# 64-row passes of three units in one group on a shared ring of six banks, with contiguous weight parts and an on-chip identity

## The chip, the cores and the metric

The kernel runs on one core of a Trainium2 chip. The core has four engines that compute: TensorE (PE in the profile; its weight loads have a row of their own, PEld), VectorE (DVE), ScalarE (ACT) and GpSimd (POOL). SyncE (SP) issues the transfers, which run on sixteen DMA engines. The metric is the device time of one execution in microseconds; lower is better.

## The reference

The input is x of 2048 tokens by 448 features. It is normalized per token, and the normalized xn feeds two branches whose results are added to x.

```
xn  = layernorm(x)                                   # no scale, no shift
A   = irfft2(rfft2(xn) * (w_r + 1j * w_i))           # 2048 x 448, filter 2048 x 225
g   = xn @ W_gate;  g = g * (g > 0)                  # W_gate, W_up: 448 x 1792
B   = (g * (xn @ W_up)) @ W_down                     # W_down: 1792 x 448
out = x + A + B
```

All inputs and the output are float32.

## The kernel before

**Precision.** Every matrix product is done in float16 on TensorE, with both operands split into a high and a low part. A product takes three kinds of pass: high by high, low by high and high by low. The weights are scaled by powers of two first, which come from their sums of squares (`w_sq`, then a reduction over the partitions on GpSimd in `w_sum`, then `w_scale`, then the split in `w_hi` and `w_lo`).

**Tokens.** Tokens are handled in four chunks q (order 0, 2, 1, 3) of 512. Each chunk's normalized rows lie transposed in a tile T of nine 128-row slices: three and a half slices of high part and as many of low part, since 448 is 3.5 times 128. The first chunk is transposed by TensorE against an identity (`ln_tp`, L338), the others by a transposing DMA (`ln_dma`, L332).

**The gated branch.** The 1792 hidden features are 14 slabs f of 128, in groups of 5, 5 and 4. A unit is one pair (f, q): gate and up for 128 features and 512 tokens, accumulated over the 3.5 slices. That is 20 passes over 128 rows (`gu_full`, L714) and, for the last half slice, two passes over 64 rows (`gu_half`, L721): the up one uses rows 64 to 127 of the array, the gate one rows 0 to 63. Passes of the two row halves can run side by side. Units are therefore taken in pairs: the first unit of a pair runs its 20 full passes, then four half passes follow, two that open its mate and two that finish itself (`gu_halves`), and then the mate runs its 20 full passes. After each unit `gu_post` empties the banks: ScalarE takes the rectified gate (`gu_relu`, L751), VectorE multiplies it by up (`gu_times`, L755), ScalarE and VectorE split the product into high and low (L759, L763). When all units of a group and a chunk are done, four down rounds follow (`dn_mm`, L782), each of 128 tokens and three passes per slab; VectorE adds each to the result (`dn_post`, L788).

**The banks.** The accumulators have eight banks: two tiles of two banks for gate and up (`gu`), two banks for down rounds (`dn`) and two for everything else (`fx`: transposes and Fourier passes).

**The spectral branch.** It is a list of background steps (`bg`): a Fourier transform over the features and one over part of the tokens as passes on TensorE (L360, L392), butterflies on VectorE, the filter, and all of it back (L611, L632). Between a spectrum's mirrored rows there are swaps through SBUF by DMA (L547, L548). Each step has a cost by a table in the kernel, and after each unit `run_bg` issues as many steps as a share of the unit's time allows. The share (`load`) is found by halving, such that all steps fit between the sixth unit and `last_gu`.

**What sets the order.** The opening, up to the first chunk's units, is a list of names written out by hand (`OPENING`), and each engine runs its part of it in that order. Names that matter here: `lx` loads a token tile in the normalization's layout, `lw` the next part of gate or up weights, `lid` the identity, `st` takes a tile's statistics (L256), `rs` computes the reciprocal deviation (L272 to L277), `wsc` the scale of a weight part, `hp` issues the half passes. After the opening a scheduler orders each engine's instructions ahead of the run by priority and by a modelled time; units are written in program order, posts with a raised priority. A tile of a ring takes a free bank, and an instruction that needs one waits until the bank's last reader is done.

Of the kernel before, what the change touches and what calls it, by code (L numbers as in the profile page):

```python
# [30 lines left out]
lx0 lx4 lw lid lw lx8 lx12 lw lw lw lw lx2 lx10 lx6 lx14 lwd0 lwd1 lwd2 lwd3 lwd4 warm st0 st4 sqA rsA hi4  # L31
xn4 xn0 wsqW0g0 cp4 st8 hi0 parW0g0 st12 wsqW0g1 cp0 tpA0 lo0 tpA4 kw1 wscW0g0 sqB tpB0 kw6 parW0g1 wsqW1g0
rsB whiW0g0 vevB0 lo4 wsqW1g1 xn12 tpB4 kw3 hi8 parW1 wscW0g1 xn8 whiW0g1 cp8 vevA0 vevA4 hi12 tpA8 vevB4
hh10 hh00 lo8 wsqW2g1 cp12 tpA12 hl00 lo12 aevA12 tpB8 aevA8 hl10 wloW0g0 lw aevB8 tpB12 wscW1 lh00 aevB12
wloW0g1 lw lfd hh01 hh11 whiW1g0 st2 lh01 lh10 whiW1g1 hl01 wloW1g0 lw hl11 wsqW2g0 cl0 cl4 wloW1g1 lw ly0 ly4 ly8
ly12 lh11 wsqW3g0 st10 parW2 hp0 st14 wsqW3g1 gu1g0 st6 wdq0 parW3 cl8 cl12 wscW2 sqC wscW3 whiW2g0 rsC gu1g1 re0
wloW2g0 whiW3g1 tm0 whiW2g1 xn6 wsqW4g0 xn2 gu2g0 dt0 dt4 wloW2g1 hi2 dt8 dt12 re1 xn10 gh0 wloW3g1 whiW3g0 tm1 gu2g1 wdq1
wloW3g0 hi10 xn14 lo2 hi14 hi6 cp14 hp2 wsqW4g1 cp2 lo6 gu3g0 cp10 cl2 dm2 lo14 re2 parW4 wdq2 cp6 wscW4 tm2
whiW4g0 cl14 dm14 lo10 wdq4 gu3g1 wloW4g0 gh1 cl10 dm10 gl0 whiW4g1 gl1 cl6 dm6 gu4g0 re3 wloW4g1 wdq3 tm3 wdp gh3
wdsc gh2 gu4g1 gl2 wdh1 wdh2 wdl1 wdh0 wdl2 hp4 gl3 re4 wdh3 tm4 wdl0 gh4 wdh4 gl4 wdl3 wdl4  # L40
# [37 lines left out]
def _constants():  # L78
# [57 lines left out]
    ident = np.eye(128, dtype=np.float16)  # L136
    return dict(ident=ident, c_fd=c_fd, c_fm=c_fm, c_im=c_im, c_row=np.ascontiguousarray(c_row),
# [4 lines left out]
def tile_gfnet_reglu(ctx: ExitStack, tc: tile.TileContext, x, xr, wgu, wd, wf, wrow, ident, c_fd, c_fm, c_im, c_row, c_id,  # L142
# [10 lines left out]
    def fx():  # L153
        return psum.tile([128, 512], F32, name="fx", bufs=2)
# [77 lines left out]
    def load_w(f, g, eng=nc.sync):  # L232
        wst[f, g] = mt([128, 4, 128], F32, "wst", 8)
        eng.dma_start(wst[f, g], wgu[f, :, g])
# [18 lines left out]
    def ln_stats(q, j):  # L253
        n2 = q + 4 * j
        st = ft([128, 6], F32, "bst", 2)
        V.bn_stats(st, xr_t[n2])  # L256
        if j == 0:
            mv[q] = ft([128, 4, 2], F32, "mv", 2)
        V.bn_aggr(mv[q][:, j, :], st)

    rst = {}
# [7 lines left out]
    def ln_rstd(q, js=(0, 1, 2, 3), bias=False):  # L269
        w, m = rst[q, js[0]]  # L270
        sd, r0, t, r, nm = (w[:, i] for i in range(5))
        V.reciprocal(r0, sd)  # L272
        V.scalar_tensor_tensor(t, m[:, :, 1], 1e-5, r0, op0=OP.add, op1=OP.mult)
        V.scalar_tensor_tensor(t, t, -0.5 * 2048, r0, op0=OP.mult, op1=OP.mult)
        V.scalar_tensor_tensor(r, t, 1.5 * 2048, r0, op0=OP.add, op1=OP.mult)
        if bias:
            V.scalar_tensor_tensor(nm, m[:, :, 0], -1.0, r, op0=OP.mult, op1=OP.mult)  # L277
        for i, j in enumerate(js):
            rst[q, j] = r[:, i:i + 1], nm[:, i:i + 1], m[:, i, 0:1]
# [10 lines left out]
    def ln_xn(n2):  # L290
        xn_b[n2] = free.pop(0)
        xn[n2] = xn_b[n2].rearrange("p g c k -> p (g c k)")[:, 0:D]
        r, _, mean = rst[n2 % 4, n2 // 4]
        V.tensor_scalar(xn[n2], xr_t[n2], mean, r, op0=OP.subtract, op1=OP.mult)

    def ln_hi(n2, fused=False):
        new_tt(n2)
        o = tt[n2].rearrange("p a b -> p (a b)")[:, 0:D]
        r, nm, _ = rst[n2 % 4, n2 // 4]
# [34 lines left out]
    def ln_tp(n2, tiles):  # L334
        if n2 not in tp:
            tp[n2] = fx().bitcast(F16).rearrange("p (a b) -> p a b", b=128)
# [11 lines left out]

    zps, eo, X, Xh, yps, cur = {}, {}, {}, {}, {}, {}

    def f_dft(n2):
        q, j = n2 % 4, n2 // 4
        js = slice(128 * j, 128 * (j + 1))
        ps = fx()
# [33 lines left out]
    def f_sdft(n2):  # L388
        y = yps[n2] = fx()[:, 0:XW].rearrange("p (g c k) -> p g c k", g=4, c=2)
# [177 lines left out]
    def row_dft(d):  # L567
        y = state["rowps"] = fx()
# [35 lines left out]
    def i_sdft(n2):  # L604
        ps = fx()
# [20 lines left out]
    def i_ddft(n2):  # L626
        ps = fx()
# [25 lines left out]

    def w_scale(f, gs=(0, 1)):
        sc = mt([128, 2], F32, "wsc", 6)
        e = eg[:, f, gs[0]:gs[-1] + 1]
        half_exponent(e, state["wm", f][:, 1, gs[0]:gs[-1] + 1])
        shift_exponent(sc[:, 0:len(gs)], e, -1, 188)
# [49 lines left out]
    def gu_open(f, q):  # L708
        hps[f, q] = psum.tile([128, 2, 512], F32, name="gu", bufs=2)

    def gu_full(f, q, gs, cs, start, stop, seq=SEQ):
        for g in gs:
            for i, (a, b) in enumerate(seq):
                last["P"] = P.matmul(hps[f, q][:, g, cs], wt[f, g][:, a, :], Tq[q][:, b, cs],  # L714
                                     start=(start and i == 0), stop=(stop and i == len(seq) - 1)).ins

    def gu_half(f, q, g, start, prev):
# [3 lines left out]
        m = P.matmul(hps[f, q][:, g, 0:512], wt[f, g][rows, 7, :], Tq[q][rows, b, :], start=start, stop=not start).ins  # L721
# [7 lines left out]
    def gu_unit(f, q, mate):  # L729
# [7 lines left out]
        gu_halves(f, q, mate)  # L737
# [11 lines left out]
    def gu_relu(f, q):  # L749
        g1s[f, q] = mt([128, 512], F32, "g1", 3)  # L750
        last["A"] = A.activation(g1s[f, q], hps[f, q][:, 0, :], AF.Relu, scale=2.0 ** -22).ins  # L751

    def gu_times(f, q):
        g1 = g1s[f, q]
        last["V"] = V.scalar_tensor_tensor(g1, hps[f, q][:, 1, :], 2.0 ** -22, g1, op0=OP.mult, op1=OP.mult).ins  # L755
# [201 lines left out]
    gseq = [("gu", g, f, q) for g, fs in enumerate(groups) for q in CHUNKS for f in fs]  # L957
    units, pend = [], []
    for k, u in enumerate(gseq):
        units.append(u)  # L960
        if k % 2 and pend:
# [5 lines left out]
    mates = {u: v for u, v in zip(gseq[::2], gseq[1::2])}  # L967
# [222 lines left out]
```

## Time and profile before

| what | value |
|---|---|
| median of 3 runs | 448.41 us (447.95 to 448.84) |
| span of the profiled execution | 446.9 us |
| granted TensorE clock | 1.000 |
| moved by DMA | 39.66 MB, mean 89 GB/s |
| full gate and up passes, L714 | 1140 |
| half passes, L721 | 112 |
| down passes, L782 | 672 |

The profile is of one execution by the hardware profiler. Its page gives busy times of the engines, the span in 40 slices, the chain of work that ended last, followed back from the last instruction, and the costliest groups of instructions. In a group's line stands the source line, the engine, the operation, what it writes and reads, the count, then busy time, the mean length of one in ns, and the idle time of the engine just before. Further views are the chain in order of time, the waits (who waited for whom: total, times, longest), the timeline, and busy times by window. A TensorE pass's recorded length is longer than its distance to the next, as passes are pipelined; costs of passes are therefore read as distances or from the chain.

### The profile page before, as it was taken

Reading aid. Unit: us, or ns where it says so; the run is one execution under the profiler, and the core shown is the slowest. Engines: PE = TensorE matmul, PEld = TensorE weight load, DVE = VectorE, ACT = ScalarE, POOL = GpSimd, SP = SyncE. Lnnn points to the kernel's source line nnn. Section 1 sums busy time; section 2 is a strip of 40 time slices with the busy share of each in tenths; the row PEclk is TensorE's granted clock in tenths of the full one; section 3 lists DMA queues with packets and bytes.
Section 4 is the critical chain, followed back from the end, with each engine's and each line's share of the span. In section 5 each row is a group of like instructions: output and inputs, shape, how many; then the busy total and the mean of one; then the engine's idle time right before and its main releaser. Section 6 shows DMA issues by size and latency. Waiting matters only on the chain.

```text
span 446.9 us, 7057 instructions
## 1 busy us (share of the span) xinstructions
PE 437.4 (98%) x2618; PEld 217.6 (49%) x2618; DVE 373.0 (83%) x801; ACT 178.7 (40%) x365; POOL 35.5 (8%) x100
## 2 busy tenths in 40 slices
PE   7999999999999999999999999999999999999996
PEld 2543545444545444444444444444444456546564
DVE  5988696998859989899999999896997998656474
ACT  5886242451543666043224145434142242233230
POOL 2431031040000150000000010000000000000000
PEclk9999999999999999999999999999999999999999
DMA  7919976041001261431220021000001332121113
GB/s 243 362 38 266 359 243 118 1 94 38 0 14 61 96 219 37 129 103 64 82 77 11 1 83 54 0 13 0 14 0 42 106 96 74 54 76 53 64 43 123
DMA packets 36827, 39.66 MB, mean 89 GB/s; under 512 B 17799, under 2 KB 32185, under 8 KB 36793
## 3 DMA queue, kind: packets, MB, share of 16 engines
q1 hardware_dynamic: 36792, 39.21, 28.1%
q8 instruction: 20, 0.33, 0.3%
q14 instruction: 15, 0.11, 0.1%
HBM read 24.45 MB, written 3.67 MB: 63 GB/s over the span
## 4 chain that ended last, share of the span: by engine, by line
PE 84%; DVE 7%; DMA 4%; ACT 1%; issue 1%; POOL 1%; SPq 1%; DVEq 0%; ACTq 0%
PE gu L714 47%; PE dn L782 27%; PE gu L721 3%; PE fx L360 2%; PE fx L392 2%; DMA sw<-y 2%; PE fx L611 2%; PE fx L632 1%; DMA y<-in_xr 1%; DVE g L755 1%; DMA T<-tt 1%; DVE bst L256 1%; DVE wt L668 1%; DVE xy L788 1%; DVE y L553 1%
## 5 line engine op out<-in xcount | busy, mean ns | idle before, releaser
L714 PE MATMUL gu<-T,wt 128*128 128x512 f16 (+1 forms) x1140 | 256.1, 376 | 0.0
L714 PEld LDWEIGHTS <-wt 128*128 128x128 f16 x1140 | 108.6, 98 | 129.9 <-issue 9.3
L782 PE MATMUL dn<-wdt,h 128*128 128x448 f16 x672 | 136.4, 352 | 0.0
L782 PEld LDWEIGHTS <-h 128*128 128x128 f16 x672 | 64.8, 98 | 60.5
L751 ACT ACTIVATE g<-gu 128x512 f32<-128x512 f32 x56 | 33.2, 594 | 111.0 <-PE gu L721 75.3
L759 ACT ACTIVATE h<-g 128x512 f16<-128x512 f32 x56 | 35.0, 626 | 52.8 <-DVE g L755 52.7
L755 DVE SCALAR_TENSOR_TENSOR g<-gu,g 128x512 f32<-128x512 f32 x56 | 38.3, 684 | 10.3 <-ACT g L751 10.2
L788 DVE SCALAR_TENSOR_TENSOR xy<-dn,dsc,xy 128x448 f32<-128x448 f32 x48 | 32.5, 678 | 15.5 <-PE dn L782 15.3
L763 DVE TENSOR_TENSOR h<-g,h 128x512 f16<-128x512 f32 x56 | 38.2, 684 | 4.9 <-ACT h L759 4.8
L664 ACT ACTIVATE wt<-wst,wsc 128x512 f16<-128x512 f32 x28 | 19.1, 716 | 15.7 <-DVE wsc L204 15.7
L197 POOL PARTITION_ALL_REDUCE wm<-wm x15 | 7.9, 523 | 159.2 <-ACT junk L194 159.2
L668 DVE SCALAR_TENSOR_TENSOR wt<-wst,wsc,wt 128x512 f16<-128x512 f32 x28 | 20.4, 744 | 0.0
L637 DVE SCALAR_TENSOR_TENSOR xy<-fx,fsc,xy 128x448 f32<-128x448 f32 x16 | 10.8, 679 | 10.1 <-PE fx L632 10.1
L721 PE MATMUL gu<-T,wt 64*128 64x512 f16 x112 | 17.0, 381 | 1.7 <-DVE g L755 0.8
L399 DVE TENSOR_TENSOR y<-y 128x456 f32<-128x456 f32 x22 | 13.9, 630 | 4.7 <-DMA row<-y 4.5
L194 ACT ACTIVATE junk<-wst 128x512 bf16<-128x512 f32 x28 | 17.4, 622 | 0.3
L553 DVE TENSOR_TENSOR y<-y,sw 128x456 f32<-128x456 f32 x16 | 10.0, 626 | 8.5 <-DMA sw<-y 8.5
L595 ACT ACTIVATE vt<-y,fsc 128x912 f16<-128x912 f32 x8 | 8.4, 1052 | 20.7 <-PE fx L611 12.3
L618 ACT ACTIVATE wf<-fx 114x512 f16<-114x512 f32 x16 | 9.4, 587 | 17.2 <-PE fx L611 17.0
L398 DVE TENSOR_TENSOR y<-y 128x456 f32<-128x456 f32 x22 | 13.8, 626 | 0.2
L611 PEld LDWEIGHTS <-vt 128*128 128x128 f16 x192 | 12.0, 98 | 3.3
L611 PE MATMUL fx<-wf,vt 128*128 128x128 f16 x192 | 13.2, 219 | 0.0
(115 smaller groups left out, 430.6 us busy)
## 6 DMA issues: line engine op xcount, KB each, us to landing
sw<-y SPq DMA_DIRECT2D x32, 224.4 KB
wst<-in_wgu SPq DMA_DIRECT2D x28, 256.0 KB
wf<-in_wf SPq DMA_DIRECT2D x8, 456.0 KB
y<-in_xr SPq DMA_DIRECT2D x16, 224.0 KB
xy<-in_x SPq DMA_DIRECT2D x16, 224.0 KB
out<-xy SPq DMA_DIRECT2D x16, 224.0 KB
wdst<-in_wd SPq DMA_DIRECT2D x14, 224.0 KB
fm<-in_c_fm SPq DMA_DIRECT2D x8, 128.0 KB
```

The costliest lines, as they stand in the source:

```text
L194: A.activation(o, src, AF.Square, scale=SQ, accum_out=acc)
L611: P.matmul(o, v[:, h, w], m[:, c, :], start=(i == 0), stop=(i == 2), skip_group_check=True)
L664: A.activation(w[:, 0:4, :], wst[f, g], AF.Copy, scale=wsc[f, g])
L668: V.scalar_tensor_tensor(w[:, 4:8, :], st, sc, w[:, 0:4, :], op0=OP.mult, op1=OP.subtract)
L714: last["P"] = P.matmul(hps[f, q][:, g, cs], wt[f, g][:, a, :], Tq[q][:, b, cs], start=(start and i == 0), stop=(stop and i == len(seq) - 1 ...
L721: m = P.matmul(hps[f, q][:, g, 0:512], wt[f, g][rows, 7, :], Tq[q][rows, b, :], start=start, stop=not start).ins
L751: last["A"] = A.activation(g1s[f, q], hps[f, q][:, 0, :], AF.Relu, scale=2.0 ** -22).ins
L755: last["V"] = V.scalar_tensor_tensor(g1, hps[f, q][:, 1, :], 2.0 ** -22, g1, op0=OP.mult, op1=OP.mult).ins
L759: A.activation(ht[f, q][:, 0, :], g1s[f, q], AF.Copy)
L763: V.tensor_tensor(h[:, 1, :], g1s.pop((f, q)), h[:, 0, :], op=OP.subtract)
L782: last["P"] = P.matmul(ps[:, 0:D], ht[f, q][:, a, js], wdt[f][:, b, :], start=(i == 0), stop=(i == n - 1)).ins
L788: last["V"] = V.scalar_tensor_tensor(xy[:, n2, :], dps[n2][:, 0:D], dsc[:, g:g + 1], xy[:, n2, :], op0=OP.mult, op1=OP.add).ins
```

## The change

It has four parts.

**Groups of six half passes.** The 56 units are cut into runs of two or three: two, two, sixteen times three, two, two. The first unit of a run opens all its mates: after its full passes come two half passes for each mate and two of its own. The down rounds of a group and a chunk are placed behind the first mate that follows. In the order of instructions, full passes that are issued after a group of half passes are kept behind it.

```diff
-    mates = {u: v for u, v in zip(gseq[::2], gseq[1::2])}
+    mates, inner, k = {}, set(), 0
+    for n in [2, 2] + [3] * 16 + [2, 2]:
+        mates[gseq[k]] = gseq[k + 1:k + n]
+        inner.update(gseq[k + 1:k + n])
+        k += n
...
-        if k % 2 and pend:
+        if u in inner and pend:
             units += pend
...
-    def gu_halves(f, q, mate):
-        gu_open(*mate)
+    def gu_halves(f, q, mates):
         m = last["P"]
-        for i in range(4):
+        vs = [v[2:] for v in mates] + [(f, q)]
+        for i in range(2 * len(vs)):
+            v = vs[i // 2]
+            if i % 2 == 0 and v != (f, q):
+                gu_open(*v)
+                opened.add(v)
             with tc.high_priority(offset=2000 if i else 0):
-                m = gu_half(*((f, q) if i > 1 else mate), 1 - i % 2, i < 2, m)
-        opened.add(mate)
+                m = gu_half(*v, 1 - i % 2, v != (f, q), m)
+        last["half"] = m
```

**A ring of six banks.** Gate and up take one bank each, and down rounds draw from the same six.

```diff
-    def fx():
-        return psum.tile([128, 512], F32, name="fx", bufs=2)
+    RINGS = {'gu': ('gu', 6), 'dn': ('gu', 6), 'fx': ('fx', 2)}
+
+    def bank(name="fx"):
+        tag, n = RINGS[name]
+        return psum.tile([128, 512], F32, name=name, tag=tag, bufs=n)
...
-        hps[f, q] = psum.tile([128, 2, 512], F32, name="gu", bufs=2)
+        hps[f, q] = [bank("gu") for g in range(2)]
...
-        ps = psum.tile([128, 512], F32, name="dn", bufs=2)
+        ps = bank("dn")
```

**Weights and identity.** The host lays gate and up out by slab and kind, so that one part (128 rows of 2 KB) is contiguous in HBM; before, gate and up rows alternated. The identity is no longer an input: GpSimd makes it behind the fill of the warm-up tile, and `lid` leaves the opening's list.

```diff
-        eng.dma_start(wst[f, g], wgu[f, :, g])
+        eng.dma_start(wst[f, g], wgu[f, g])
...
-    wgu = np.ascontiguousarray(np.stack([wtiles(B_W_gate), wtiles(B_W_up)], axis=2))
+    wgu = np.ascontiguousarray(np.stack([wtiles(B_W_gate), wtiles(B_W_up)], axis=1))
...
         G.memset(warm, 0.0)
-        wps = psum.tile([128, 512], F32, name="dn", bufs=2)
+        G.memset(id_t, 0.0)
+        G.affine_select(id_t, id_t, pattern=[[-1, 128]], compare_op=OP.not_equal, fill=1.0, base=0, channel_multiplier=1)
+        wps = bank("dn")
```

The entries `rs` and `wsc` of the opening are cut into single steps (`rsA.0` to `rsA.4`, `wscW0g0.0` and `.1` and so on), each step standing where the whole entry stood; apart from `lid` the order of the opening is the same. In the main part `w_scale` is cut in two likewise (`w_exp` and `w_scale`), both issued at the same unit.

**Pace.** Background steps must fit into two gate/up units fewer.

```diff
-    last_gu = max(gus) - 6
+    last_gu = max(gus) - 8
```

More of the change, by code (lines that the diff above doesn't have):

```diff
@@ L335, in ln_tp @@
         if n2 not in tp:
-            tp[n2] = fx().bitcast(F16).rearrange("p (a b) -> p a b", b=128)
+            tp[n2] = bank().bitcast(F16).rearrange("p (a b) -> p a b", b=128)
         for a in tiles:
@@ L353, in f_dft @@
         js = slice(128 * j, 128 * (j + 1))
-        ps = fx()
+        ps = bank()
         T = Tq[q]
@@ L567, in row_dft @@
     def row_dft(d):
-        y = state["rowps"] = fx()
+        y = state["rowps"] = bank()
         for d in ((0, 1), (2,))[d]:
@@ L604, in i_sdft @@
     def i_sdft(n2):
-        ps = fx()
+        ps = bank()
         v, m = vt[n2 % 8][:, n2 // 8], im_t[n2 % 8][:, n2 // 8]
@@ L626, in i_ddft @@
     def i_ddft(n2):
-        ps = fx()
+        ps = bank()
         h = pgh[n2]
@@ L713, in gu_full @@
             for i, (a, b) in enumerate(seq):
-                last["P"] = P.matmul(hps[f, q][:, g, cs], wt[f, g][:, a, :], Tq[q][:, b, cs],
+                m = last["P"] = P.matmul(hps[f, q][g][:, cs], wt[f, g][:, a, :], Tq[q][:, b, cs],
                                      start=(start and i == 0), stop=(stop and i == len(seq) - 1)).ins
+                if "opened" in state and "half" in last:
+                    tc.add_manual_dep(m, last["half"].name, NOSYNC, reason="half passes stand together")
     def gu_half(f, q, g, start, prev):
         rows, b = TOP[g]
-        m = P.matmul(hps[f, q][:, g, 0:512], wt[f, g][rows, 7, :], Tq[q][rows, b, :], start=start, stop=not start).ins
+        m = P.matmul(hps[f, q][g], wt[f, g][rows, 7, :], Tq[q][rows, b, :], start=start, stop=not start).ins
         if "opened" in state:
@@ L727, in tile_gfnet_reglu, with gu_unit @@
     opened = set()
-    def gu_unit(f, q, mate):
+    def gu_unit(f, q, mates):
         gs, cs = (0, 1), slice(0, 512)
@@ L1033, in tile_gfnet_reglu @@
             piece("sq" + tag, ln_sd, q, js)
-            piece("rs" + tag, ln_rstd, q, js, c == 0)
+            for i in range(4 + (c == 0)):
+                piece(f"rs{tag}.{i}", ln_rstd, q, js, c == 0, range(i, i + 1))
         for j in range(4):
@@ L1046, in gu_slab @@
     def gu_slab(f, g):
-        if f % 2 == 0 and g == 0:
+        first = ("gu", 0, f, q) in mates
+        if first and g == 0:
             gu_open(f, q)
-        gu_full(f, q, (g,), slice(0, 512), f % 2 == 0, f % 2 == 1)
+        gu_full(f, q, (g,), slice(0, 512), first, not first)
     for f in groups[0]:
@@ L1117, in tile_gfnet_reglu @@
             run_bg(until=marks["T", q])
-            gu_unit(f, q, (mates.get(u) or (0, 0, None, None))[2:])
+            gu_unit(f, q, mates.get(u))
         else:
```

78 lines of the change are left out of this document (38 added, 40 removed).

## The prediction

> **What bounds the kernel now.** All durations come from one profiled execution with a span of 446.9 us; the median of the runs is 448.41 us, so 1.5 us lie outside the span, and I leave them as they are. I read the page's busy times first, then its chain of work, and then asked what TensorE waits for.
>
> ```profile
> PE 437.4 (98%) x2618; PEld 217.6 (49%) x2618; DVE 373.0 (83%) x801; ACT 178.7 (40%) x365; POOL 35.5 (8%) x100
> PE 84%; DVE 7%; DMA 4%; ACT 1%; issue 1%; POOL 1%; SPq 1%; DVEq 0%; ACTq 0%
> ```
>
> TensorE is busy nearly throughout and carries 84% of the chain that ended last. A busy TensorE isn't yet one that streams densely, so the view of its waits comes next; of its seven rows these two are the only ones on the gate and up passes over 0.2 us:
>
> ```profile
> PE gu L721 <- DVE g L755: 0.8, 1, 0.8
> PE gu L721 <- DMA T<-tt: 0.8, 1, 0.8
> ```
>
> Both fall on the 64-row passes (L721). Everything else that can be won in the middle must therefore come from the passes themselves. The chain in order of time (start, length, what) shows what a group of four of them costs:
>
> ```profile
> 108.23 0.54 PE gu L721 x4
> 108.77 4.42 PE gu L714 x20
> 113.19 1.21 PE fx L360 x24
> 114.40 4.32 PE gu L714 x20
> 118.72 0.54 PE gu L721 x4
> 119.26 1.32 PE fx L360 x24
> ```
>
> Twenty full passes take 4.32 us, 0.216 us each. The same twenty take 4.42 us right behind a group, and the 24 Fourier passes 1.32 instead of 1.21 us: a change of row mode costs about 0.10 us more than the group's own 0.54 us. So a group costs 0.64 us, where its two pairs, each pair running side by side in the two halves of the array, need 2 x 0.216 = 0.43 us. The overhead is **0.21 us per group**. The timeline shows why:
>
> ```profile
> 118.65 0.11 PEld L721 LDWEIGHTS <-wt 64*128 64x128 f16 x4 [0.42 <-issue]
> 118.65 0.61 PE L721 MATMUL gu<-T,wt 64*128 64x512 f16 x4
> ...
> 119.18 0.47 PEld L360 LDWEIGHTS <-T 128*128 128x128 f16 x9 [0.42 <-issue]
> ```
>
> The weight load stands idle 0.42 us on entry and again on exit; elsewhere it runs ahead under the passes.
>
> **Part 1: three units in a group.**
>
> ```profile
> L721 PE MATMUL gu<-T,wt 64*128 64x512 f16 x112 | 17.0, 381 | 1.7 <-DVE g L755 0.8
> ```
>
> The 56 gate/up units make 112 such passes, 28 groups of four. By the list in the change (two twos, sixteen threes, two twos) they become 4 groups of four and 16 of six, again 112 passes. A group of six adds one pair: 0.64 + 0.22 = 0.86 us. Before: 28 x 0.64 = 17.9 us. After: 16 x 0.86 + 4 x 0.64 = 16.3 us. **Gain 1.6 us**, all of it on TensorE, which sets the end.
>
> The third pair's weights are the unknown. No row shows a third pair. One end: its loads hide, as do those of the second pair in the quoted timeline row (four loads in 0.11 us, all at the start) and those of the full passes. The other end: both loads stand bare, about the 0.11 us of that row, 16 x 0.11 = 1.8 us, which takes the gain away. I take nothing, because the second pair of the same mode is the nearest row.
>
> The Trainium skill, "TensorE: Matmul & The Clock Gate", section "Part 3: Packing small matmuls — row/col tiling", says that a weight load overlaps a running matmul only when it goes to another row group. By that rule the third pair could load nothing while the second pair fills both groups, and the sum would be that of rival A. The trace disagrees as far as it reaches: the second pair's loads are recorded beside the first pair's run.
>
> **Part 2: ring of six banks.** Before, gate and up shared a two-bank tile with two buffers, and the down passes had two banks of their own. Now both draw single banks from six. The gate bank comes free after L751 alone instead of after L755, and a down round may hold up to four banks. Against that, at each group of six all six banks belong to gate and up.
>
> ```profile
> L751 ACT ACTIVATE g<-gu 128x512 f32<-128x512 f32 x56 | 33.2, 594 | 111.0 <-PE gu L721 75.3
> ...
> L755 DVE SCALAR_TENSOR_TENSOR g<-gu,g 128x512 f32<-128x512 f32 x56 | 38.3, 684 | 10.3 <-ACT g L751 10.2
> L788 DVE SCALAR_TENSOR_TENSOR xy<-dn,dsc,xy 128x448 f32<-128x448 f32 x48 | 32.5, 678 | 15.5 <-PE dn L782 15.3
> ```
>
> The last unit of one group must be emptied (0.59 + 0.68 = 1.3 us) while the first unit of the next runs its 4.32 us, which leaves 3.0 us for queues. That is the same slack as now, and it failed once in 28 groups: VectorE stood behind a swap transfer, and the group waited 0.81 us.
>
> ```profile
> 397.66 0.63 DVE L553 TENSOR_TENSOR y<-y,sw 128x456 f32<-128x456 f32 x1 [4.27 <-DMA sw<-y]
> ...
> 398.75 0.69 DVE L755 SCALAR_TENSOR_TENSOR g<-gu,g 128x512 f32<-128x512 f32 x1
> ...
> 399.49 0.61 PE L721 MATMUL gu<-T,wt 64*128 64x512 f16 x4 [0.81 <-DVE g L755]
> ```
>
> What is queued behind such a wait is every later TensorE pass. I count no gain and no loss: the swap waits remain, there are fewer groups to hit, but each needs more banks. The bounds are -0.8 us (this wait goes) and the price of rival C.
>
> **Part 3: the opening.** The order written out by hand loses one entry, the load of the identity; splitting the rsqrt steps and the weight scale into several entries leaves their order as it was, so I cost that at nothing. The chain of the opening:
>
> ```profile
> 2.14 0.43 SPq L1022
> ...
> 2.62 0.43 SPq L234
> ...
> 3.09 4.74 DMA y<-in_xr
> ```
>
> The identity's issue (L1022) holds SyncE from 2.14 to 2.62 us. Without it the second weight part and the third and fourth token tiles are issued 0.48 us earlier. VectorE waits for that third tile:
>
> ```profile
> 7.85 0.63 DVE L256 BATCH_NORM_STATS2 bst<-y 128x6 f32<-128x448 f32 x1 [0.80 <-DMA y<-in_xr]
> ```
>
> ```profile
> 10.00:20.00 10.00, 9.00 (x80) 6.16 (x81) 9.66 (x32) 9.16 (x21) 3.51 (x10) 1.00 1.02 379
> ```
>
> It can win at most these 0.80 us, and at least nothing, if the transfers and not the issue set the landing. From there to 20 us VectorE is full (9.66 of 10 us in the second row), so a shift is handed on. Contiguous parts act on the same landing. In windows over the transfers (last two columns: DMA share, GB/s):
>
> ```profile
> 3.50:5.00 1.50, 1.50 (x5) 0.51 (x4) 1.32 (x4) 0.07 (x1) 0.00 (x0) 1.00 0.80 201
> ...
> 8.10:9.60 1.50, 0.72 (x7) 0.39 (x7) 1.43 (x5) 0.92 (x4) 0.78 (x3) 1.00 0.89 279
> 11.50:14.00 2.50, 1.65 (x14) 0.88 (x14) 2.47 (x10) 1.95 (x5) 0.99 (x3) 1.00 1.05 402
> 16.60:18.00 1.40, 1.40 (x15) 1.27 (x13) 1.33 (x4) 1.40 (x4) 0.00 (x0) 1.00 1.05 384
> ```
>
> Weight parts move at 201 and 279 GB/s in the first 10 us, at 384 at 16.6 us; the down weights and tokens at 402. Since strided parts reach 384 later, I put the early slowness down to starting up, not to the stride, and give contiguity nothing by itself. For the opening I take **0.4 us**, half of the bound and a little under the slot of 0.48.
>
> The identity now costs GpSimd two instructions behind the fill of the warm-up tile.
>
> ```profile
> 0.96 0.52 POOL L1077 MEMSET warm<- 128x512 f16 x1
> ...
> 7.06 0.22 POOL L307 COPY tt<-tt 128x48 f16<-128x48 f16 x1 [5.57 <-ACT tt L301]
> ...
> 8.32 0.51 PE L338 MATMUL fx<-id_t,tt 128*128 128x128 f16 x6 [0.85 <-ACT tt L301]
> ```
>
> A quarter of that fill is 0.13 us; the select has no row and lies between the copy's 0.22 and, for twice the fill, 1.0 us. GpSimd's idle 5.57 us hide both, and the first reader comes at 8.32. Without the cover TensorE's first transposes would wait by the excess.
>
> **Part 4: pace.** Background work is spread over two gate/up units fewer, by the kernel's own table about 2% more per unit. VectorE has no room for that in the middle:
>
> ```profile
> 190.00:200.00 10.00, 10.00 (x52) 4.48 (x50) 9.97 (x24) 4.65 (x8) 0.00 (x0) 1.00 0.30 96
> ...
> 420.00:430.00 10.00, 10.00 (x98) 6.16 (x97) 5.75 (x9) 4.00 (x7) 0.00 (x0) 1.00 0.07 24
> ```
>
> VectorE is busy 9.97 of 10 us there, 5.75 near the end, where TensorE is full anyway. So earlier background work shortens nothing by itself: what doesn't fit slides on, and gate/up evacuations have priority in the order. Nothing, with rival C as the bad end.
>
> **Sum:** 446.9 - 1.6 - 0.4 = 444.9 us of span, **446.4 us** as a time.
>
> **Rivals.**
>
> A, the third pair's weights aren't hidden: +1.8 us, so 448.2 us. For it: in these passes both row groups are occupied. Against it: the four loads in 0.11 us.
>
> B, the groups don't stay together, so the change doesn't do what it says. A group needs four banks for its two mates; if the second mate's aren't free when the first's are, the scheduler can set other passes between, and the row mode changes twice more, 0.21 us as worked out. Half of the sixteen broken costs 1.7 us: 448.1 us. All: 449.8. For it: only the first pass of a group has no raised priority, and the later ones need banks of their own now. Against it: the mates' banks are freed some 3 us before they are needed.
>
> C, slower: **down rounds in front of a group**. In the order of before, ten of the 28 groups stand right behind down passes; the first and the last of the ten in the timeline:
>
> ```profile
> 156.53 0.35 PE L782 MATMUL dn<-wdt,h 128*128 128x448 f16 x1
> 156.81 0.39 PE L721 MATMUL gu<-T,wt 64*128 64x512 f16 x2
> ...
> 363.30 0.54 PE L782 MATMUL dn<-wdt,h 128*128 128x448 f16 x2
> 363.77 0.39 PE L721 MATMUL gu<-T,wt 64*128 64x512 f16 x2
> ```
>
> On their own two banks that costs nothing; on the common ring the second mate waits until the last down bank is emptied, 0.68 us of L788 and what VectorE has in hand, some 1.0 us. TensorE stands, and all behind it. In proportion that would meet seven of 20 groups. Four of these waits give 446.4 + 4.0 = 450.4 us; from three on the kernel is slower. Against it: the new order is made for the new ring, and a down round now follows the second unit with a whole unit behind it.
>
> The Trainium skill, "TensorEngine Tiling (Array Packing)", section "Gotcha 1: PSUM Pressure", warns that row tiling raises the demand for PSUM banks. That speaks against six passes on six banks. The trace bears it out so far in one wait of 0.81 us in 28 groups.
>
> D, better: the wait at 399 us goes too and the opening gives its whole 0.80: 445.2 us.
>
> **Chances.** The forecast 0.53, D 0.10, A 0.07, B 0.13, C 0.17. A measurement of this kernel tells apart about 0.2%, 0.9 us: faster means below 447.5. The forecast and D lie there, B and A mostly within, C and a wholly broken B beyond. Faster 0.63, same 0.19, slower 0.18. The range runs from 444.6 (D, and the transposes' 0.8 us wait for T partly gone) to 449.8 (B whole, C with three waits), leaving out C's longer half and little below.
>
> **What would show it.** Right: 20 runs of L721 passes, sixteen of six in about 0.76 us each; 0.42 us idle of the weight load 40 times instead of 56; no wait at L721 on VectorE beyond one; the third token tile's statistics starting near 7.4 us; no load of the identity. Wrong: pairs of a six more than 0.23 us apart (A), L721 passes in more than 20 runs (B), L721 waiting on L788 (C), or statistics still at 7.85 us. If the opening moves but its gain is missing at 40 us, another wait took it: then the transposes' transfer into T is the first suspect.

## The result and the profile after

| what | before | after |
|---|---|---|
| median of the runs | 448.41 us (447.95 to 448.84) | 465.44 us (462.63 to 466.59) |
| ratio | | 1.037, interval 1.035 to 1.039 |
| span of the profiled execution | 446.9 us | 462.9 us |
| third group of half passes starts at | 38.87 us | 50.71 us |
| from there to the last TensorE pass | 404.04 us | 408.18 us |

The kernel became slower by 17 us, far outside the range. One execution in the whole study, the traced one of run f3 below, took 573.8 us at a granted clock of 0.754, and the ratios leave it out. The last two rows split the 16.0 us between the spans: 11.84 us are lost before the third group of half passes, 4.14 us after it. Lines have moved: half passes are L721 as before, but full passes are L712, down passes L786, gate times up L759, the transposes' copies on GpSimd L306.

The page of after, busy times and the chain by engine:

```profile
PE 439.7 (95%) x2618; PEld 220.3 (48%) x2618; DVE 375.6 (81%) x801; ACT 177.4 (38%) x365; POOL 40.1 (9%) x102
PE 63%; DVE 17%; DMA 8%; issue 6%; ACT 3%; SPq 2%; POOL 1%; DVEq 0%; ACTq 0%; POOLq 0%
```

TensorE falls from 98% to 95% of a longer span and from 84% to 63% of the chain. Its waits in after (who waits for whom: us in total, times, longest) say for whom:

```profile
PE fx L336 <- POOL tt L306: 8.6, 1, 8.6
PE fx L608 <- DVE wf L619: 3.1, 3, 1.9
PE fx L336 <- POOL id_t L1092: 2.6, 1, 2.6
PE gu L721 <- DVE g L759: 1.7, 1, 1.7
...
PE fx L357 <- DVE eo L369: 0.5, 1, 0.5
```

**The opening.** Two of these waits are on GpSimd, 8.6 and 2.6 us, together 11.2. GpSimd's timeline in after (start, length, instruction, idle time before it and what ended that):

```profile
1.42 0.20 POOL L1091 MEMSET id_t<- 128x128 f16 x1
9.96 0.28 POOL L1092 TENSOR_SCALAR_AFFINE_SELECT id_t<-id_t 128x128 f16<-128x128 f16 x1 [8.33 <-issue]
...
10.38 0.23 POOL L306 COPY tt<-tt 128x64 f16<-128x64 f16 x1
19.05 0.40 POOL L190 PARTITION_ALL_REDUCE wm<-wm  x1 [8.44 <-issue]
```

The select itself takes 0.28 us, but GpSimd stands still for 8.33 us in front of it and for 8.44 us in front of the first sum over partitions behind it. "issue" means that no semaphore ended the wait: GpSimd waited for nothing that the profile shows. Before, the same sum came after 0.25 us:

```profile
7.70 0.39 POOL L197 PARTITION_ALL_REDUCE wm<-wm  x1 [0.25 <-ACT junk L194]
```

Everything in the opening hangs on these two. VectorE needs the sum for the scale of the weights, TensorE the identity and GpSimd's copies for its transposes; after, VectorE and TensorE:

```profile
19.48 0.15 DVE L193 TENSOR_SCALAR eg<-wm 128x1 uint32<-128x1 uint32 x1 [9.91 <-POOL wm L190]
19.85 0.29 PE L336 MATMUL fx<-id_t,tt 128*128 128x128 f16 x1 [8.62 <-POOL tt L306]
```

The third group of half passes, in after:

```profile
50.71 0.82 PE L721 MATMUL gu<-T,wt 64*128 64x512 f16 x6 [1.16 <-DMA T<-tt]
```

It was at 38.87 us before. Windows of after (length; busy time and count for PE, PEld, DVE, ACT, POOL; granted clock; DMA share; GB/s) show the hole, and a clock that is lower through it and behind it:

```profile
10.00:20.00 10.00, 1.08 (x13) 0.79 (x13) 0.45 (x4) 0.15 (x1) 1.56 (x7) 0.61 0.74 274
20.00:30.00 10.00, 10.00 (x69) 6.76 (x68) 8.01 (x26) 7.35 (x15) 3.42 (x10) 0.71 0.27 77
```

**The groups of six.** They are what the prediction said. The chain of after in order of time:

```profile
260.85 4.32 PE gu L712 x20
265.17 0.75 PE gu L721 x6
265.92 13.06 PE gu L712 x60
```

Six half passes take 0.75 us; the sixty full passes behind them take 13.06 where 60 x 0.216 = 12.96, so 0.10 us of exit. With this exit a group of six costs 0.85 us, against 0.86 worked out. The trace has 20 groups, as planned.

**The middle.** The 4.14 us are these, by distances between starts of TensorE's passes:

| term | us |
|---|---|
| shorter groups (28 became 20), as predicted | -1.6 |
| the wait of before at 399 us is gone | -0.9 |
| one wait inside a group of six at 199 us | +2.0 |
| five stalls at Fourier passes (127, 368, 396, 406 and 407 us) | +4.5 |
| sum | +4.0 of 4.1 |

The longest of the five stalls, in after (VectorE's and TensorE's rows):

```profile
403.65 0.63 DVE L550 TENSOR_TENSOR y<-y,sw 128x456 f32<-128x456 f32 x1 [4.04 <-DMA sw<-y]
...
408.15 0.68 DVE L619 SCALAR_TENSOR_TENSOR wf<-fx,wf 114x512 f16<-114x512 f32 x1
...
408.89 0.84 PE L608 MATMUL fx<-wf,vt 128*128 128x128 f16 x12 [1.86 <-DVE wf L619]
```

VectorE takes its instructions in a fixed order. The butterfly at L550 waits 4.04 us for a swap transfer, and what follows stands almost without a gap until 408 us: the evacuations, the next inverse step and in the end L619, which empties a Fourier bank that TensorE needs. VectorE's waits on swaps, before and after:

```profile
DVE y L553 <- DMA sw<-y: 8.5, 3, 4.3
```

```profile
DVE y L550 <- DMA sw<-y: 14.6, 6, 4.0
```

### The profile page after: what moved, and what is told of

Read it like the earlier page. It is cut to its first block, busy times and chain, and to the rows that moved or that the text cites. A ratio compares the mean times of both kernels' runs of the same rounds, so it can differ in the third digit from the quotient of the medians.

```text
span 462.9 us, 7090 instructions
## 1 busy us (share of the span) xinstructions
PE 439.7 (95%) x2618; PEld 220.3 (48%) x2618; DVE 375.6 (81%) x801; ACT 177.4 (38%) x365; POOL 40.1 (9%) x102
## 4 chain that ended last, share of the span: by engine, by line
PE 63%; DVE 17%; DMA 8%; issue 6%; ACT 3%; SPq 2%; POOL 1%; DVEq 0%; ACTq 0%; POOLq 0%
PE gu L712 35%; PE dn L786 19%; DMA sw<-y 6%; PE gu L721 2%; DVE g L759 2%; PE fx L389 2%; PE fx L629 1%; DVE xy L792 1%; PE fx L357 1%; PE fx L608 1%; DVE y L551 1%; ACT junk L187 1%; DVE y L419 1%; SPq L330 1%; DMA row<-y 1%
## 5 line engine op out<-in xcount | busy, mean ns | idle before, releaser
L712 PE MATMUL gu<-T,wt 128*128 128x512 f16 (+1 forms) x1140 | 253.5, 376 | 0.0
L712 PEld LDWEIGHTS <-wt 128*128 128x128 f16 x1140 | 109.3, 98 | 128.8 <-issue 6.8
L786 PE MATMUL dn<-wdt,h 128*128 128x448 f16 x672 | 132.4, 353 | 0.0
L786 PEld LDWEIGHTS <-h 128*128 128x128 f16 x672 | 65.0, 98 | 59.4
L759 DVE SCALAR_TENSOR_TENSOR g<-gu,g 128x512 f32<-128x512 f32 x56 | 38.3, 684 | 10.9 <-ACT g L755 6.8
L550 DVE TENSOR_TENSOR y<-y,sw 128x456 f32<-128x456 f32 x16 | 10.0, 627 | 16.1 <-DMA sw<-y 14.6
L396 DVE TENSOR_TENSOR y<-y 128x456 f32<-128x456 f32 x22 | 13.8, 629 | 6.8 <-DMA row<-y 6.4
L721 PE MATMUL gu<-T,wt 64*128 64x512 f16 x112 | 16.1, 380 | 3.1 <-DVE g L759 1.7
L380 ACT ACTIVATE Xh<-X 128x912 f16<-128x912 f32 x8 | 7.7, 962 | 21.6 <-DVE X L378 21.6
L336 PE MATMUL fx<-id_t,tt 128*128 128x128 f16 x32 | 3.6, 244 | 11.2 <-POOL tt L306 8.6
## 6 DMA issues: line engine op xcount, KB each, us to landing
wf<-in_wf SPq DMA_DIRECT2D x8, 456.0 KB
```

Of the source, the lines that this page charges most:

```text
L712: m = last["P"] = P.matmul(hps[f, q][g][:, cs], wt[f, g][:, a, :], Tq[q][:, b, cs], start=(start and i == 0), stop=(stop and i == len(seq) ...
L721: m = P.matmul(hps[f, q][g], wt[f, g][rows, 7, :], Tq[q][rows, b, :], start=start, stop=not start).ins
L759: last["V"] = V.scalar_tensor_tensor(g1, hps[f, q][1], 2.0 ** -22, g1, op0=OP.mult, op1=OP.mult).ins
L786: last["P"] = P.matmul(ps[:, 0:D], ht[f, q][:, a, js], wdt[f][:, b, :], start=(i == 0), stop=(i == n - 1)).ins
```

## The experiments

Four questions: what the identity costs, whether the pace, the ring or the groups make the middle longer, whether it is instead any change of order at all, and whether the groups of six keep their gain. Beside the runs e, f, g and h, before was measured again on the same chip: 448.7, 448.6, 448.8 and 448.6 us. The ratio is taken over the executions, not from the two medians.

| label | kernel | median, us | ratio to before, interval |
|---|---|---|---|
| e1_after_loaded_identity | after, identity loaded | 453.76 | 1.0113 (1.0081 to 1.0145) |
| e2_before_made_identity | before, identity made | 460.29 | 1.0256 (1.0241 to 1.0271) |
| e3_loaded_pace6 | e1, pace of before | 456.44 | 1.0180 (1.0162 to 1.0199) |
| e4_loaded_fours | e1, groups of four | 454.59 | 1.0130 (1.0115 to 1.0145) |
| f1_before_pace8 | before, pace of after | 453.53 | 1.0098 (1.0075 to 1.0120) |
| f2_before_ring | before, ring of six | 453.63 | 1.0110 (1.0094 to 1.0126) |
| f3_before_contiguous | before, contiguous parts | 448.36 | 0.9987 (0.9978 to 0.9996) |
| f4_contiguous_act_identity | f3, identity issued by ScalarE | 447.70 | 0.9980 (0.9971 to 0.9990) |
| g1_before_share_up | before, share x 1.003 | 452.17 | 1.0090 (1.0064 to 1.0116) |
| g2_before_share_down | before, share x 0.997 | 453.11 | 1.0096 (1.0082 to 1.0111) |
| g3_before_later_pair | before, inverse pairs later | 450.60 | 1.0041 (1.0028 to 1.0054) |
| g4_six_act_later_pair | sixes, inverse pairs later | 451.30 | 1.0057 (1.0041 to 1.0074) |
| h1_six_share_up | sixes, share x 1.003 | 456.00 | 1.0165 (1.0118 to 1.0213) |
| h2_six_share_down | sixes, share x 0.997 | 451.72 | 1.0089 (1.0059 to 1.0120) |
| h3_six_pace7 | sixes, pace 7 | 450.81 | 1.0049 (1.0034 to 1.0064) |
| h4_six_later_pair_pace6 | sixes, pairs later, pace 6 | 451.78 | 1.0077 (1.0062 to 1.0092) |

"Sixes" is after with the identity loaded by ScalarE's queue.

### The identity: undone in after, done alone in before

```diff
 e1, against after
-lx0 lx4 lw lw lx8 ...
+lx0 lx4 lw lid lw lx8 ...
+    pieces = {"lid": lambda: nc.sync.dma_start(id_t, ident), ...
-        G.memset(id_t, 0.0)
-        G.affine_select(id_t, id_t, pattern=[[-1, 128]], compare_op=OP.not_equal, fill=1.0, base=0, channel_multiplier=1)
```

> The changed kernel, with the identity loaded by SyncE at its old place again; the orders on TensorE, VectorE and ScalarE are those of the changed kernel. Theory 1 (the identity made on GpSimd costs two code loads, the 8.3 us of idle before the select and the 8.4 us before the first reduction over partitions in the changed kernel's trace, of which some 11.8 us reach TensorE at its third group of half passes, 50.71 against 38.87 us): 465.4 - 11.8 = 453.6 us, GpSimd's idle before the first reduction back at about 0.25 us. Rival (the opening's delay is taken back later, or groups and ring cost most): still above 458 us.

```diff
 e2, against before
-lx0 lx4 lw lid lw lx8 ...
+lx0 lx4 lw lw lx8 ...
+        G.memset(id_t, 0.0)
+        G.affine_select(id_t, id_t, pattern=[[-1, 128]], compare_op=OP.not_equal, fill=1.0, base=0, channel_multiplier=1)
```

> The kernel before, with only the identity made on GpSimd and its load left out; the orders on TensorE, VectorE and ScalarE are those of the kernel before. Theory 1: 448.4 + 11.8 = 460.2 us, with the same two idle stretches of about 8 us on GpSimd. Rival (the reduction's code load was there before too and the select only moved it, or the later stages absorb the delay): 448 to 452 us.

Both came out as expected. Undone, the third group of half passes is back at 38.70 us (e1's timeline):

```profile
38.70 0.82 PE L722 MATMUL gu<-T,wt 64*128 64x512 f16 x6 [0.70 <-DMA T<-tt]
```

Done alone, it stands at 50.82 us, and GpSimd shows the same two holes (e2's timeline):

```profile
9.91 0.28 POOL L1078 TENSOR_SCALAR_AFFINE_SELECT id_t<-id_t 128x128 f16<-128x128 f16 x1 [8.28 <-issue]
...
19.39 0.40 POOL L196 PARTITION_ALL_REDUCE wm<-wm  x1 [8.83 <-issue]
```

e1's orders on TensorE, VectorE and ScalarE are those of after, e2's those of before, so nothing else differs. The identity costs 460.29 - 448.69 = 11.6 us in before and 465.44 - 453.76 = 11.7 us in after (in the latter pair the two kernels were not measured side by side). The second hole comes with the first: without the select, no sum waits so.

The Trainium skill, "GPSIMD Engine Reference", section "2.1 Instruction dispatch", says that the first call of a freshly loaded GpSimd routine pays some 6 us for loading its code, and that no instruction in the profile shows it. The trace agrees in kind, with 8.3 us in front of the select, and it shows a second idle stretch of 8.4 us in front of the first sum over partitions behind it. That the time goes into loading code is a reading by the page; the runs show only idle time that comes and goes with the select.

### The middle: pace, ring, groups

What stays is e1's 5.1 us over before. The first theory was the pace: eight units' reserve in place of six pushes background work into a full VectorE.

```diff
 e3, against e1
-    last_gu = max(gus) - 8
+    last_gu = max(gus) - 6
```

> As the changed kernel with the identity loaded, and the pace of the kernel before (six units instead of eight). Theory 1's second half says that the pace puts VectorE's background work in front of the emptying of banks (a product of gate and up came 8 us after its gate in the changed kernel's trace at 192 to 200 us), so most of the 4 to 5 us left go: 447 to 449.5 us. Rival (the ring and the groups of six make the stalls): as with the pace of eight, about 453 us.

```diff
 e4, against e1
-    for n in [2, 2] + [3] * 16 + [2, 2]:
+    for n in [2] * 28:
```

> As the changed kernel with the identity loaded, and groups of four half passes throughout, still on the ring of six banks and with the pace of eight. If the six banks held at once by a group of six make the stalls, they go and the eight changes of row mode come back: 453.6 - 5 + 1.6 = about 450 us. If pace or order make them, they stay: 454 to 456 us.

The theory of pace falls: with the old pace e3 is 2.7 us slower than e1, longer than either forecast for it. It also has 22 groups instead of 20. Groups of four on the new ring (e4) lose as much as groups of six, as one of the two forecasts had it. Then the parts were put into before, each alone:

```diff
 f1, against before
-    last_gu = max(gus) - 6
+    last_gu = max(gus) - 8
```

> The kernel before with the changed pace alone (eight units instead of six). Theory 2 (the ring of six gives the scheduler an order in which TensorE meets passes that wait for VectorE, and VectorE stands in its own order behind a swap's transfer): 448 to 449.5 us. Rival P (the pace does it): 452 to 454 us. Rival O (the order of before is a good one among many, and any edit that shuffles it loses): 451 to 455 us here and in the ring's run alike.

f2 takes the code of after for banks, steps and groups into before, with twenty-eight groups of four, the loaded identity, alternating weight parts and the old pace:

```diff
 f2, against before
+    RINGS = {'gu': ('gu', 6), 'dn': ('gu', 6), 'fx': ('fx', 2)}
...
-        hps[f, q] = psum.tile([128, 2, 512], F32, name="gu", bufs=2)
+        hps[f, q] = [bank("gu") for g in range(2)]
...
-        ps = psum.tile([128, 512], F32, name="dn", bufs=2)
+        ps = bank("dn")
...
+    for n in [2] * 28:
```

> The kernel before with the ring of six banks alone: groups of four, loaded identity, alternating weight parts, pace of six. Theory 2: 452 to 455 us, with TensorE stalls of 4 to 6 us at full and inverse passes between 340 and 440 us. Rival P: 448 to 449.5 us. Rival O: 451 to 455 us.

With the ring, f2 also takes over the cut steps of `rs` and `wsc` and the rule that keeps later full passes behind a group. Pace and ring cost 4.9 and 5.0 us, each as much as all together in e1. Costs that don't add up are hardly prices of the parts. f2's trace shows where its time goes, and it is the same place (VectorE and TensorE):

```profile
398.97 0.63 DVE L551 TENSOR_TENSOR y<-y,sw 128x456 f32<-128x456 f32 x1 [3.28 <-DMA sw<-y]
```

```profile
367.21 0.75 PE L630 MATMUL fx<-idc_t,wf 114*128 114x112 f16 x12 [1.32 <-DVE wf L620]
404.46 0.75 PE L630 MATMUL fx<-idc_t,wf 114*128 114x112 f16 x12 [0.67 <-DVE wf L620]
```

### The opening's other two edits

```diff
 f3, against before
-        eng.dma_start(wst[f, g], wgu[f, :, g])
+        eng.dma_start(wst[f, g], wgu[f, g])
...
-    wgu = np.ascontiguousarray(np.stack([wtiles(B_W_gate), wtiles(B_W_up)], axis=2))
+    wgu = np.ascontiguousarray(np.stack([wtiles(B_W_gate), wtiles(B_W_up)], axis=1))
```

> The kernel before with contiguous weight parts alone; the orders on all engines but SyncE's numbering stay. The prediction's step (contiguity gives nothing by itself): 448.0 to 448.8 us, the third token tile's statistics still near 7.85 us. Rival (the alternating rows slowed the early parts, 201 and 279 GB/s): statistics up to 0.8 us earlier, 447.6 to 448.0 us.

```diff
 f4, against f3
-lx0 lx4 lw lid lw lx8 ...
+lid lx0 lx4 lw lw lx8 ...
-    pieces = {"lid": lambda: nc.sync.dma_start(id_t, ident), ...
+    pieces = {"lid": lambda: nc.scalar.dma_start(id_t, ident), ...
```

> As the run with contiguous parts, and the identity's load issued by ScalarE at the start, so that SyncE's queue loses it as in the change but GpSimd does nothing new. The prediction's opening step (the issue slot of 0.48 us, 0.4 us of gain, at most 0.80): statistics of the third tile at 7.05 to 7.4 us, the third group of half passes 0.4 to 0.8 us earlier than at 38.87 us, 447.6 to 448.1 us. Rival (the gain is lost before the transposing transfer into T): the statistics move, the third group stays at 38.7 us or later, 448.4 us.

Contiguous parts give 0.1%, with an interval that barely leaves out nothing. f3's trace isn't read, so whether its statistics stay near 7.85 us isn't shown. In f4 SyncE's list is without the identity, as in after, but the identity is loaded, by a queue that is free at the start. f4's timeline, VectorE and TensorE:

```profile
7.37 0.63 DVE L256 BATCH_NORM_STATS2 bst<-y 128x6 f32<-128x448 f32 x1
```

```profile
38.36 0.61 PE L721 MATMUL gu<-T,wt 64*128 64x512 f16 x4 [0.67 <-DMA T<-tt]
...
398.53 0.61 PE L721 MATMUL gu<-T,wt 64*128 64x512 f16 x4 [0.36 <-DVE g L755]
```

The third token tile's statistics start 0.48 us earlier than the 7.85 of before, the third group 0.51 us earlier, and the wait at 399 us shrinks from 0.81 to 0.36. The spans differ by 1.0 us, and the medians by 0.9. f4 stays within all three of its forecasts. At 447.7 us it is the best version of the study, 0.2% below before.

### Any other order

Pace, ring and groups all change the order that the scheduler finds, and with it what stands on VectorE behind a swap. The theory O: the order of before happens to be a good one, and any other loses some us, whatever made it; the times of f1 and f2 lie where it had them. The smallest nudge changes no pass, bank or group:

```diff
 g1, against before (g2: 0.997)
-    load[0] = hi
+    load[0] = hi * 1.003
```

> The kernel before with the share of background work raised by 0.3%, which means nothing by itself but gives the scheduler another order from the first chunk on. Rival O (the order of before is a good one, any other loses at the swaps): 450 to 454 us. Theory 2 (ring and pace each have a cost of their own): 448.2 to 449 us.

> The kernel before with the share lowered by 0.3%, another order from the middle on. Rival O: 450 to 454 us. Theory 2: 448.2 to 449 us.

A share moved by 0.3% either way costs 3.4 and 4.4 us. In g1 one wait holds 1.9 of the 3.0 us between the spans (VectorE, then TensorE):

```profile
400.73 0.63 DVE L553 TENSOR_TENSOR y<-y,sw 128x456 f32<-128x456 f32 x1 [4.60 <-DMA sw<-y]
...
401.83 0.68 DVE L755 SCALAR_TENSOR_TENSOR g<-gu,g 128x512 f32<-128x512 f32 x1
```

```profile
402.56 0.61 PE L721 MATMUL gu<-T,wt 64*128 64x512 f16 x4 [2.75 <-DVE g L755]
```

It is the wait that the prediction quotes from before at 399.49 us, 0.81 us there and 2.75 here. In g2 the same kind is spread over six waits on swaps, 12.7 us of VectorE's time. So O holds: the order alone costs 3.4 to 4.4 us. The other traces fit. The three in which TensorE's and VectorE's instructions stand in the order of before (before, e2, f4) take 403.6 to 404.0 us from the third group of half passes to the last pass; the fourteen with another order take 405.3 to 413.7.

If the swaps are the place, more time between a swap and its reader should mend it. In g3 the inverse pairs come one step later in the list, with a fourth buffer for the swaps, so that the inverse ends a step later too:

```diff
 g3, against before
-NSW = 3
+NSW = 4
...
-    for t in range(16 + 6 + len(il)):
+    for t in range(16 + 8 + len(il)):
...
-            if 0 <= m - 2 < 8:
-                add(1.26, i_pair, m - 2)
+            if 0 <= m - 3 < 8:
+                add(1.26, i_pair, m - 3)
```

> The kernel before, with the use of a swapped pair in the inverse part one step later behind its swap, and a fourth swap buffer. Theory 3 (TensorE's stalls come from VectorE standing in order behind a swap's transfer, which takes longer than the order allows): VectorE's waits on swaps between 340 and 440 us shrink from 8.5 us to 3 or less, the group at 399 us no longer waits 0.81 us, 447.4 to 448.2 us. Rival (the waits only move): 448.4 us or more.

g4 has the same edits in sixes, with the pace of after:

> The changed kernel (groups of six, ring, pace of eight, contiguous parts), with the identity loaded by ScalarE and the later use of a swapped pair. Theory 3: of the 453.8 us of the run with a loaded identity, 0.7 us go in the opening and some 3 to 4 us of stalls between 340 and 440 us: 449 to 450 us, and below 448 if the stall in the group of six near 187 us goes too. Rival (the ring itself makes the stalls): 452 to 453 us.

VectorE's waits on swaps fall to 4.7 us in g3 and 6.3 in g4, the stall at 399 us is gone, and TensorE is busy through 340 to 440 us in g4. Neither is faster than before: in g3 the rival's time came out, and g4 lies between its two forecasts. In g3 the pairs' own chain now ends later and stalls TensorE between 428 and 445 us, by some 2.7 us; a wait removed at one end of the list came back at the other. g4 loses its gain elsewhere: in two waits for Fourier passes near 115 us (1.7 us, with a granted clock of 0.66 from 115 to 120 us), in a wait inside a group at 189 us, and in 5.0 us behind the start of the last pass, against 3.9 in before. The waits on swaps alone don't set the time either: h2 and h4 below take 451.7 and 451.8 us with 15.7 and 2.9 us of them.

### Do the groups of six keep their gain?

Theory S: the groups of six keep the 1.6 us that they save. Rival M: waits for a mate's bank inside a group take it back. The last four kernels draw the order anew with groups of six, by the same nudges. Four such draws with groups of four (f1, f2, g1, g2) have a mean of 453.1 us, or 452.4 less the 0.7 us that the expectations allow for the opening; e4, a fifth, lies at 454.6.

```diff
 h1, against sixes (h2: 0.997)
-    load[0] = hi
+    load[0] = hi * 1.003
```

> After with the identity loaded on ScalarE's queue and the share of background work multiplied by 1.003. Three kernels of before with another order gave 452.2, 453.1 and 453.5; the earlier opening takes 0.7 us off (f4 beside before): 452.2 as the middle for an order drawn anew. Theory S, the groups of six keep their 1.64 us: a draw between 449.9 and 451.2, with the mean of the four kernels of this call near 450.6. Rival M, six banks cost about as much in waits for a mate's bank inside a group as the longer groups save: the mean of the four lies at 452 or above, and in their traces PE at L721 waits behind VectorE's L759 for over 1 us in most of them.

> As h1 with the share multiplied by 0.997. Theory S: 449.9 to 451.2, with PE at L721 waiting under 0.5 us behind VectorE. Rival M: 452 or above, with a wait of over 1 us inside a group. Either way VectorE's waits on the swap transfer come to 10 us or more, as in every other order, where the time is above 450.

```diff
 h3, against sixes
-    last_gu = max(gus) - 8
+    last_gu = max(gus) - 7
```

> After with the identity loaded on ScalarE's queue and background work paced to end seven half passes early in place of eight. Theory S: 449.9 to 451.2. Rival M: 452 or above. If seven were the pace that suits groups of six (a theory of pace, which e3 at six has already hurt), below 447.7, the time of f4.

h4 is g4 with `max(gus) - 6`:

> After with ScalarE's identity load, the inverse pairs one step later, and a pace of six. The stalls at the swaps before 400 us are gone as in g3 and g4, and come back near the end, as there: theory S 449 to 450.5 (g3's 450.6 less 0.7 less 1.6 would be 448.3 at best), rival M 451 to 452.5 as g4's 451.3. Below 447.7 would make it the best version.

The four have a mean of 452.6 us, where M had it, so on average nothing is left of 1.6 us. None is below f4. Single times scatter from 450.8 to 456.0, too far for the mean alone to decide: h3 lies in the range of S, h2 in neither. The traces are clearer. TensorE waits inside a group in every one of the eight profiled kernels with groups of six, the longest time always between 185 and 200 us, and never inside one in the nine with groups of four whose traces were read:

| kernel | after | e1 | e3 | g4 | h1 | h2 | h3 | h4 |
|---|---|---|---|---|---|---|---|---|
| distance between third and fourth pass, us | 2.03 | 1.67 | 2.25 | 1.95 | 2.11 | 2.01 | 1.70 | 2.20 |

In h2 two more groups wait, at 267 and 292 us, with distances of 0.4 and 0.8 us. Rival B came too: in e3, h2, h3 and h4 two groups of six, and in g4 one, are cut in halves with Fourier passes between, and one such half in h3 waits 0.9 us for its bank. In after, whose 20 groups are whole, three passes run, and the fourth stands until L759 has emptied its bank:

```profile
198.62 0.60 PE L721 MATMUL gu<-T,wt 64*128 64x512 f16 x3
...
200.14 0.68 DVE L759 SCALAR_TENSOR_TENSOR g<-gu,g 128x512 f32<-128x512 f32 x1
...
200.86 0.63 ACT L763 ACTIVATE h<-g 128x512 f16<-128x512 f32 x1 [8.01 <-DVE g L759]
200.88 0.59 PE L721 MATMUL gu<-T,wt 64*128 64x512 f16 x3 [1.66 <-DVE g L759]
```

ScalarE had taken the gate of that unit at 192.25 us, so L759 comes 7.3 us after the gate is done. VectorE had waited 2.97 us for a swap until 191.23, and from there it runs butterflies, filter steps and two additions of down rounds without a gap. In h3 it is the same instruction (L760 there), at 188.47 us. With groups of four the lateness isn't always free either: in f1 a full pass waits 1.0 us for such a product near 192 us. One wait inside a group takes 1.7 to 2.2 us, as much as sixteen longer groups save. So the traces speak for M. That the groups would keep their 1.6 us without this wait isn't shown, as no run takes it away.

h1 shows one cost more. Windows of its TensorE (length, busy, granted clock, DMA share, GB/s):

```profile
188.00:190.00 2.00, 0.30 (x3) 1.00 0.70 227
...
191.00:195.00 4.00, 4.00 (x12) 0.57 0.00 0
...
364.00:368.00 4.00, 4.00 (x11) 0.50 0.26 83
```

Behind a wait of 2 us the granted clock is 0.57 for 4 us, and 0.50 for as long again at 364 us behind two waits. By these figures I estimate 4 x 0.43 + 4 x 0.5 = 3.7 us, of the 6.2 us by which h1's span (456.0) is longer than h2's (449.8).

## Why the prediction was wrong

**Part 3, the failed step.** "GpSimd's idle 5.57 us hide both." The durations were near enough, 0.20 and 0.28 us. What was wrong was to price an instruction by the nearest rows' durations alone, when the trace held no such instruction: the first use has a cost of its own that no duration holds, 8.3 us in front of it and 8.4 us in front of the first sum behind it. The cover of 5.57 us would have been too short even for one. The loss is 11.6 to 11.8 us.

**Part 3, the rest.** Right in kind. The statistics of the third token tile start at 7.07 us in after, almost the whole bound of 0.80 us before the 7.85 of the kernel before; 7.4 was forecast (after's timeline):

```profile
7.07 0.63 DVE L249 BATCH_NORM_STATS2 bst<-y 128x6 f32<-128x448 f32 x1
```

The 0.4 us taken for the opening is 0.5 in f4. Contiguity was given nothing, and gives some 0.1%.

**Part 1.** Right in its mechanism and its size: 20 groups, 0.85 us for six, the third pair's loads hidden, so rival A is out. Less the listed waits, the stretch behind the third group is 1.5 us shorter than before, where 1.6 was worked out. After's timeline, passes and weight loads of one group:

```profile
239.94 0.82 PE L721 MATMUL gu<-T,wt 64*128 64x512 f16 x6
```

```profile
239.94 0.33 PEld L721 LDWEIGHTS <-wt 64*128 64x128 f16 x6 [0.42 <-issue]
```

**Part 2.** "I count no gain and no loss" failed. The bounds were the gain of 0.8 us and rival C. C had the right effect, a second mate that waits for a bank that VectorE hasn't emptied, but the wrong instruction and place: L759 behind filter work near 190 us, not L788 in front of a group. In after it came once, for 2.0 us, not four times for 1. The step that failed is the slack of 3.0 us: L759 came 7.3 us behind its gate.

**Part 4.** "Nothing, with rival C as the bad end" failed as well (with the pace as its only edit f1 takes 4.9 us more), together with the "no gain and no loss" of the swap waits. I treated the waits at the swaps as the price of a plan that stays; they are what the order decides. Before had one group that waited 0.81 us for a swap. That looked like 0.8 us still to be won, and it was a good draw: four other orders of the same passes lose 3.4 to 5.0 us. No rival covered this.

**What stays open.** Why VectorE is late near 190 us in every kernel with groups of six wasn't tried apart: no kernel had groups of four at that place alone. Nor was an order with groups of six found that keeps their 1.6 us; the best, h3, is 3.1 us behind f4. The runs of the kernels with stalls also scatter more (h1 from 453.6 to 458.0 us, before beside it from 447.9 to 448.9). In h1 this goes with the granted clock of each execution: 457.8 and 458.0 us at 0.989, 453.6 and 454.2 at 0.996. In g1 the longest (455.4 us) has the lowest clock too, 0.992; in h2 the longest (454.1 us, at 0.998) has not. So the clock can be a part of it only, and its cause isn't shown.

## What to carry to other kernels

An operation that the trace has no row for can cost more than any row suggests: try it alone on its engine, look at the idle time in front of it and in front of the next different instruction, and prefer a load on an idle queue (f4) to a clever instruction on the path. In a kernel whose engines follow a fixed order around transfers, test first what a meaningless nudge of the order costs (here 3.4 to 4.4 us for 0.3%); an edit worth less than that can't be judged by one draw. A saving on the bounding engine that takes up all buffers at once needs its partner engine on time, and one late evacuation can take back sixteen savings.

## What the runs showed of the hardware

- A GpSimd select into 128x128 took 0.28 us, with 8.3 us of idle time in front of it; the next sum over partitions had 8.4 to 8.8 us. Copies between the two (0.21 and 0.23 us) had none.
- The granted clock fell to 0.57 behind a single wait of some 2 us in h1, but stayed at 1.00 behind the 2.75 us in g1:

```profile
404.00:408.00 4.00, 4.00 (x38) 1.00 0.15 57
```

  The Trainium skill, "TensorE: Matmul & The Clock Gate", section "HAM oscillation — how this bites in real kernels", warns of gaps over about 3.4 us. Here the clock fell behind a shorter wait in h1 and stayed at 1.00 behind a longer one in g1. The length of a wait doesn't decide it: behind the same two waits near 115 us, 1.7 us together, the clock from 115 to 120 us was 0.66 in g4 and 1.00 in h1.
- Three pairs of 64-row passes ran in 0.75 us, the way in included, with the third pair's weight loads hidden; the change of row mode cost 0.10 us on the way out, for six as for four.
